# Attention with two feed-forward stages on one Trainium2 core: the second stage's w_in product by seven products instead of eight

## The chip, the cores and the metric

The kernel runs on one core of a Trainium2 chip. The time is the device time of one execution in microseconds (us); three executions were timed, and one more was profiled. TensorE (PE) multiplies, VectorE (DVE) and ScalarE (ACT) work elementwise, GpSimd (POOL) takes column maxima in the attention, and SyncE (SP) issues all DMAs, in program order.

## What is computed

A gated sum of causal attention and a memory read (4 batches, 8 heads, 576 tokens, head width 64) gives 2,304 tokens of width 512. Two feed-forward stages follow, all in float32:

```python
a = x @ w1
b = x @ w2
h = a * b @ w3
x = h @ w_out              # first stage: 512 -> 1024 -> 1024 -> 512

h = x @ w_in               # second stage: 512 -> 2048
sp = log1p(exp(h))
g = h * tanh(sp)           # Mish
return g @ w_out           # 2048 -> 512
```

## The kernel before

Everything is recorded first as a list of operations (`op`, line 104), each with an engine, a cost and the buffers that it reads and writes. `Recorder.schedule` (line 140) then sets the order: it plays the list through with the planner's costs, and on each engine takes the ready operation with the best key. On TensorE the key is the place in the record, plus `GB` = 300 for fill work; on the others it weighs the length of the chain that hangs on an operation against the place in the record. Buffers are given by name (tag) from rings of fixed length (`BUFS`, line 343); an operation that opens a buffer waits until the ring has one free. The order that comes out is fixed in the program: each engine, and the DMA queue of SP, goes through its list in order.

SBUF is divided in rooms. R1 and A1 serve the attention and the first feed-forward stage; R2 and A2 take their space when those are done (`rec.follow`, lines 1096 and 1105). A2 (tags f, s) opens when the attention ends, R2 when the first stage ends.

Every float32 operand is split in two float32r tiles, a rounded part H and the rest L, and one product is three matmuls (H·H, H·L, L·H in `HL`, line 768). The split is a cast on ScalarE and a subtraction on VectorE (`split`, line 875; `lo`, line 379). The weights of the second stage come as 64-bit numbers: a raw load of 512 KB into a buffer s, then one operation on ScalarE and two on VectorE turn 128 rows into float32 (`conv`, line 737; `conv2`, line 864). Two such row groups make one pair i of 8 (`NP2`).

The second stage works on chunks of 256 tokens (`CT`), 9 of them (`NC`). For each chunk and each pair i:

- an **h block** (`h_blk`, line 913) multiplies the activations of the chunk with pair i of w_in: 2 row groups x 4 parts of the depth x 3 matmuls of 256 columns = 24 matmuls into one PSUM bank;
- a **g block** (`g_blk`, line 929) takes Mish from PSUM (ScalarE), forms three sums and differences (VectorE), and splits the seven pieces that result (one cast, one subtraction of 896 columns);
- an **out block** (`fin`, line 946) multiplies them with w_out. It already uses seven products of half-size blocks in place of eight: 7 x 3 = 21 matmuls of 256 columns (`PRODUCTS`, line 944), summed over the pairs in four banks. `combine` (line 884) forms the combinations of w_out for it, four operations of 256 columns on VectorE and two splits (1,024 and 768 columns) per pair, in the first chunk.

h blocks and out blocks alternate on TensorE, the out block `LA` = 2 pairs behind. When a chunk is complete, `out_blk` (line 962) puts its four banks together and stores 2 x 256 KB. `load_x2` (line 899) loads and splits the next chunk's activations from DRAM (x2d).

The loads for this stage are recorded between the last units of the first stage (lines 1097 to 1104): 16 row groups of w_out and the first 10 of w_in, then 6 more beside the splits of w_in. All converted weights stay in SBUF in the ring f of 13.

Of the kernel before, what the change touches and what calls it, by code (L numbers as in the profile page):

```python
# [8 lines left out]
F32 = mybir.dt.float32  # L9
F32R = mybir.dt.float32r  # L10
# [276 lines left out]
def t_mm(n, m=128):  # L287
    return max(n * 0.4545 + 2, m * 0.834 + 2)
# [9 lines left out]
def kernel(  # L298
# [53 lines left out]
    ROOMS = {"x": R1, "u": R1, "t": R1, "f": A2, "s": A2, "G": R2, "H": R2, "ob": R2, "m": R2}  # L352
# [521 lines left out]

    def split(n, a, H, L):
        act(n, lambda: fl(H), lambda: fl(a), [a], [H])
        lo(n, lambda: fl(L), lambda: fl(a), lambda: fl(H), [a, H], [L])

    def split_in(i):
        for d in (WH, WL):  # L880
            d[i] = buf("wE" if i < 2 else "wB" if i < 6 else "wD", [P, 2, 512], F32R)
        split(1024, WC[i], WH[i], WL[i])

    def combine(i):

        c, m = LC[i], buf("ob", [P, 3, 256])
# [5 lines left out]
        HC[i] = buf("wA", [P, 2, 512], F32R)  # L892
        LL[i] = buf("f", [P, 2, 512], F32R)
        split(1024, c, HC[i], LL[i])
        for y, d in enumerate((HM, LM)):
            d[i] = buf("m" if 2 * i + y < BUFS["m"] else "f", [P, 3, 256], F32R)
        split(768, m, HM[i], LM[i])

    def load_x2(c):
        t0 = c * CT  # L900
        need = [x for x in range(2 * B) if x * HS < t0 + CT and (x + 1) * HS > t0]
        xc[c] = []
# [10 lines left out]
    def h_blk(c, i):  # L913
        ps = gbuf()
        w = (WH[i], WL[i])
        for y in range(2):
            for j in range(KD // 2):

                def f(y=y, j=j):
                    for k in range(2):  # L920
                        for z, (a, b) in enumerate(HL):
                            kk = 2 * j + k
                            mm(ps.tile[:, y * CT:(y + 1) * CT], w[a].tile[:, y, kk * P:(kk + 1) * P], xc[c][j].tile[:, b, k * CT:(k + 1) * CT],
                               kk == z == 0, kk == KD - 1 and z == 2)

                op("pe", 6 * t_mm(CT), f, r=[WH[i], WL[i], (xc[c][j], 0), (xc[c][j], 1)], w=[ps])
        return ps

    def g_blk(ps):
        G = buf("G", [P, 8, P])  # L930
        H = buf("H", [P, 2, 7 * P], F32R)
# [7 lines left out]
        act(7 * P, lambda: H.tile[:, 0], g7, [(G, 0), (G, 1)], [(H, 0)])  # L939
        lo(7 * P, lambda: H.tile[:, 1], g7, lambda: H.tile[:, 0], [(G, 0), (G, 1), (H, 0)], [(H, 1)])  # L940
        return H


# [168 lines left out]
    load_x2(0)
    NC = NT // CT
    for c in range(NC):
        acc = [gbuf() for _ in range(4)]
        gts = {}
        LA = CFG["LA"]
        for i in range(NP2 + LA):
            if i < NP2:
                if c == 0:  # L1120
                    combine(i)
                ps = h_blk(c, i)
            if i >= LA and (c < NC - 1 or i < NP2 + LA - 2):
                fin(i - LA, gts.pop(i - LA), acc)
            if i < NP2:
                gts[i] = g_blk(ps)
            if i == NP2 - 1 and c + 1 < NC:
                load_x2(c + 1)
        for part in (PRODUCTS[:6], PRODUCTS[6:]):
            for i in sorted(gts):  # L1130
                fin(i, gts[i], acc, part)
        out_blk(c, acc)
# [56 lines left out]
```

## Time and profile before

| | us |
|---|---|
| runs shown: 942.35, 942.94, 940.69; median | 942.35 |
| the profiled execution | 944.09 |
| its span, first to last instruction | 942.3 |
| TensorE busy in the span | 928.4 |
| VectorE busy | 675.6 |
| ScalarE busy | 536.4 |
| second stage, from TensorE's first h matmul to the end of the span | 551.5 to 942.3 |

The span is what the profile's rows count from; the execution's own time is 1.8 us longer. A matmul's recorded duration (281 ns for 256 columns) is longer than the distance to the next one, since they are pipelined: durations of TensorE are read from starts. The same holds, less so, on VectorE and ScalarE.

### The profile page before, as it was taken

How to read it: one execution, taken by the hardware profiler on the slowest of the kernel's cores; microseconds unless marked ns; L12 is line 12 of the kernel's file. 1: busy time of each engine (PE TensorE's matmuls, PEld its weight loads, DVE VectorE, ACT ScalarE, POOL GpSimd, SP SyncE). 2: the span in 40 equal slices, each digit the busy share in tenths (PEclk: the TensorE clock that was granted, in tenths of full speed). 3: DMA queues.
4: the chain of work that ended last, by engine and by line, in shares of the span. 5: the costliest groups of instructions: out<-in, count | busy, mean ns of one | idle time of the engine just before them, and what ended most of it. 6: DMA issues, size and time to landing. Idle time of an engine off the chain costs nothing.

```text
span 942.3 us, 17917 instructions
## 1 busy us (share of the span) xinstructions
PE 928.4 (99%) x6936; PEld 872.1 (93%) x6936; DVE 675.6 (72%) x1574; ACT 536.4 (57%) x1070; POOL 83.8 (9%) x70
## 2 busy tenths in 40 slices
PE   9999999999999999999999999999999999999998
PEld 7455888899899999999999999999999999999997
DVE  8989998999898988987367949844444454545453
ACT  6679967888787877866255745433233333333232
POOL 2111112322211112120000000000000000000000
PEclk9999999999999999999999999999999999999999
DMA  9788563543433522311299400000001010100000
GB/s 320 263 259 292 172 178 115 178 109 94 132 91 104 146 74 85 109 28 52 64 301 328 145 26 24 19 28 23 24 23 46 1 46 1 46 23 24 1 24 23
DMA packets 50341, 95.21 MB, mean 101 GB/s; under 512 B 10992, under 2 KB 27920, under 8 KB 50256
## 3 DMA queue, kind: packets, MB, share of 16 engines
q1 hardware_dynamic: 50256, 94.07, 31.3%
q8 instruction: 54, 0.88, 0.4%
q14 instruction: 31, 0.25, 0.1%
HBM read 84.28 MB, written 9.77 MB: 100 GB/s over the span
## 4 chain that ended last, share of the span: by engine, by line
PE 76%; DVE 10%; DMA 6%; ACT 5%; issue 2%; SPq 0%; POOL 0%; DVEq 0%; ACTq 0%
PE g L367 76%; DMA Rr<-d 3%; DVE t L385 2%; DVE QK L370 2%; DMA d<-cp 1%; DVE mnl L385 1%; DVE e L385 1%; ACT t L377 1%; DVE e L370 1%; DVE g L624 1%; ACT u L750 1%; DVE x L370 1%; ACT e L377 1%; DMA cp<-d 1%; DMA ld<-in_qk_dram 1%
## 5 line engine op out<-in xcount | busy, mean ns | idle before, releaser
L370 DVE TENSOR_TENSOR H<-G,H 128x896 fp32r<-128x896 f32 x72 | 78.7, 1092 | 97.3 <-ACT H L375 97.3
L385 DVE TENSOR_TENSOR t<-g,t 128x288 f32<-128x288 f32 (+6 forms) x344 | 121.2, 380 | 21.1 <-PE g L367 17.2
L375 ACT CAST H<-G 128x896 fp32r<-128x896 f32 x72 | 67.9, 943 | 119.1 <-PE g L367 99.4
L367 PE MATMUL g<-wA,H 128*128 128x256 f32 x576 | 135.6, 281 | 0.0
L385 DVE TENSOR_TENSOR G<-G 128x128 f32<-128x128 f32 (+1 forms) x216 | 72.4, 335 | 60.3 <-ACT G L934 55.8
L644 POOL PARTITION_ALL_REDUCE t<-t x64 | 83.1, 1307 | 351.4 <-DVE t L385 293.5
L367 PE MATMUL g<-f,H 128*128 128x256 f32 x477 | 111.7, 280 | 0.0
L367 PE MATMUL g<-x,wB 128*128 128x288 f32 x768 | 109.8, 296 | 0.5 <-DVE e L385 0.5
L367 PE MATMUL g<-u,wA 128*128 128x288 f32 x768 | 110.2, 298 | 0.0
L367 PE MATMUL g<-s,wB 128*128 128x256 f32 x864 | 109.5, 282 | 0.0
L367 PEld LDWEIGHTS g<-s,wB 128*128 128x128 f32 x864 | 106.1, 188 | 0.0
L367 PEld LDWEIGHTS g<-x,wB 128*128 128x128 f32 x768 | 104.4, 188 | 1.2 <-DVE e L385 0.7
L367 PEld LDWEIGHTS g<-u,wA 128*128 128x128 f32 x768 | 104.2, 188 | 1.3 <-ACT R L375 0.2
L367 PEld LDWEIGHTS g<-wA,H 128*128 128x128 f32 x576 | 103.0, 189 | 0.0
L934 ACT ACTIVATE G<-g 128x512 f32<-128x512 f32 x72 | 43.0, 597 | 95.0 <-PE g L367 87.7
L367 PE MATMUL g<-e,V 128*65 128x320 f32 (+12 forms) x576 | 89.3, 302 | 2.5 <-DVE t L385 1.3
L367 PEld LDWEIGHTS g<-e,V 128*65 128x65 f32 (+1 forms) x576 | 66.3, 136 | 19.8 <-issue 2.2
L367 PE MATMUL g<-m,H 128*128 128x256 f32 x459 | 83.1, 281 | 0.0
L367 PEld LDWEIGHTS g<-f,H 128*128 128x128 f32 x477 | 82.1, 188 | 0.0
L367 PEld LDWEIGHTS g<-m,H 128*128 128x128 f32 x459 | 66.9, 188 | 0.0
L367 PE MATMUL g<-wB,wD 128*128 128x512 f32 x128 | 59.5, 603 | 2.8 <-DVE wB L754 1.4
L367 PE MATMUL g<-x,wE 128*128 128x288 f32 x384 | 55.8, 300 | 1.1 <-DVE t L385 0.9
(121 smaller groups left out, 1553.4 us busy)
## 6 DMA issues: line engine op xcount, KB each, us to landing
ld<-in_qk_dram SPq DMA_DIRECT2D x24, 608.0 KB
u<-in_moe_w_dram SPq DMA_DIRECT2D x26, 512.0 KB
s<-in_moe_w_out_dram SPq DMA_DIRECT2D x16, 512.0 KB
s<-in_moe_w_in_dram SPq DMA_DIRECT2D x16, 512.0 KB
Rr<-d SPq DMA_DIRECT2D x24, 288.0 KB
x2d<-t SPq DMA_DIRECT2D x16, 288.0 KB
s<-x2d SPq DMA_DIRECT2D x18, 256.0 KB
out_dram<-ob SPq DMA_DIRECT2D x18, 256.0 KB
```

What stands on the lines that cost most here:

```text
L367: nc.tensor.matmul(out=o, lhsT=lhsT, rhs=rhs, start=start, stop=stop)
L370: eng.tensor_tensor(out=o, in0=a, in1=b, op=ALU.subtract)
L375: op("act", t_act(n, psum), lambda: nc.scalar.copy(out=o(), in_=i()), r, w)
L377: op("act", t_act(n, psum) + more, lambda: nc.scalar.activation(out=o(), in_=i(), func=func, **kw), r, w)
L385: op(eng, t_dve(n) if eng == "dve" else t_pool(n), lambda: e.tensor_tensor(out=o(), in0=a(), in1=b(), op=alu), r, w)
L624: nc.vector.tensor_tensor(out=o, in0=o, in1=mv, op=ALU.add)
L644: op("pool", 430 + 2.6 * (b - a), lambda mv=mv: nc.gpsimd.partition_all_reduce(mv(), mv(), P, bass_isa.ReduceOp.max), r=[(m, x)], w=[(m, x)])
L750: op("act", t_act(512) + 100, lambda: nc.scalar.activation(out=lw(), in_=top(), func=AF.Identity, scale=2.0 ** -5, bias=frac), r=[(raw, 0) ...
L934: op("act", t_act(512, True), lambda: nc.scalar.activation(out=G.tile[:, 0:4].rearrange("p a b -> p (a b)"), in_=ps.tile, func=AF.Mish, sc ...
```

## The change

w_in too is now multiplied by seven products of half-size blocks, two chunks of 256 tokens at a time. Nine chunks are odd, so the first 256 tokens go through the old h block, and the other 2,048 in four chunks of 512 (`NS` = 4).

- `split_sums` forms four sums and differences of a pair of w_in and splits them (tiles SH, SL), beside the pair's own split.
- `load_x2s` loads 512 tokens of activations, forms four differences of 512 columns and splits seven factors (tags r and b).
- `h_seven` is a **step**: for one chunk of 512 and one pair, seven products of 2 x 3 = 6 matmuls of 256 columns into four banks; then one copy on ScalarE and four additions on VectorE (three of 512 columns, one of 256) give h in a buffer G, one Mish of 1,024 columns follows, and `store_g` writes G to DRAM.
- Both products are no longer interleaved: all steps run first, then all 72 out blocks. `g_blk` loads its 256 KB of g from DRAM, and does the rest as before.
- SBUF no longer holds all weights: `keep` writes a converted pair to DRAM, `fetch` loads it again. Kept are all 8 pairs of w_out and pairs 5 to 7 of w_in. `combine` writes the splits of w_out over the buffers that the same pair of w_in had.

The core of the diff:

```diff
-        "f": 13, "s": 4, "G": 2, "H": 2, "ob": 1, "m": 11, **CFG.get("BUFS", {}),
+        "f": 5, "s": 4, "q": 8, "b": 8, "r": 4, "G": 2, **CFG.get("BUFS", {}),
...
+    def split_sums(i, o):
+        c = WC[i]
+        for x, y, z, alu in ((3, (c, 2), (c, 3), ALU.add), (2, (c, 0), (c, 2), ALU.subtract), (0, (o, 3), (c, 0), ALU.subtract), (1, (c, 1), (o, 0), ALU.subtract)):
+            tt(256, lambda x=x: quarter(o, x), lambda y=y: quarter(*y), lambda z=z: quarter(*z), alu, [c, o], [o])
+        for d in (SH, SL):
+            d[i] = buf(side(i), [P, 2, 512], F32R)
+        split(1024, o, SH[i], SL[i])
+
+    def keep(to, src, i, swap):
+        for y in range(2):
+            conv2(to, src, i, y, 1 - y if swap else y)
+        d = ld[swap, i] = Buf(dram, [P, 1024], F32, f"kept{swap}_{i}", 1)
+        c = to[i]
+        dma(lambda: d.tile, lambda: fl(c), 524288, r=[c], w=[d])
...
+    FACTORS = [(0, 0, 0, 0), (0, 1, 1, 0), (1, 0, 1, 1), (1, 2, 2, 0), (1, 3, 2, 1), (0, 3, 3, 0), (1, 1, 3, 1)]
+
+    def h_seven(c, i, then=()):
+        G = buf("G", [P, 4, CT])
+        bank = [gbuf() for _ in range(4)]
+        for x, (d, qd, k, half) in enumerate(FACTORS):
...
+                for kk in range(2):
+                    for z, (a, b) in enumerate(HL):
+                        mm(bank[k].tile[:, CT * half:CT * half + CT], quarter(w[a], qd)[:, kk * P:kk * P + P], xc[c][x].tile[:, b, kk * CT:kk * CT + CT],
+                           kk == z == 0, kk == 1 and z == 2)
+            op("pe", 6 * t_mm(CT), f, r=[w[0], w[1], (xc[c][x], 0), (xc[c][x], 1)], w=[bank[k]])
+            if x < len(then):
+                then[x]()
...
+        act(CT, lambda: o(0), lambda: bank[0].tile[:, 0:CT], [bank[0]], [G], True)
+        tt(512, lambda: o(1, 3), lambda: pair(1), lambda: wide(0), ALU.add, [bank[1], G], [G])
+        tt(512, lambda: o(0, 4, 3), lambda: pair(2), lambda: wide(2), ALU.add, [bank[2], G], [G])
+        tt(CT, lambda: o(2), lambda: bank[2].tile[:, CT:512], lambda: o(0), ALU.add, [bank[2], G], [G])
+        tt(512, lambda: o(0, 4, 3), lambda: pair(3), lambda: o(0, 4, 3), ALU.add, [bank[3], G], [G])
+        op("act", t_act(1024), lambda: nc.scalar.activation(out=fl(G), in_=fl(G), func=AF.Mish, scale=2.0 ** -8), [G, table], [G])
+        store_g(c, i, G, 1024)
+
+    def g_blk(c, i):
+        G = buf("r", [P, 8, P])
+        H = [buf("b", [P, 7 * P], F32R) for _ in range(2)]
...
+        dma(lambda: G.tile[:, 0:4].rearrange("p a b -> p (a b)"), lambda: d.tile[:, 512 * y:512 * y + 512], 262144, r=[d], w=[(G, 0)])
...
+    loads = [lambda i=i: keep(LC, moe2_w_out, i, 1) for i in range(NP2)]
+    loads += [lambda i=i: keep(WC, moe2_w_in, i, 0) for i in range(BUFS["f"], NP2)]
+    loads += [lambda i=i, y=y: conv2(WC, moe2_w_in, i, y) for i in range(BUFS["f"]) for y in range(2)]
+    loads += [load_x2]
+    loads += [lambda i=i: split_sums(i, buf("s", [P, 2, 512])) for i in range(4)]
...
+    for i in range(NP2):
+        h_blk(i)
+        if i == 2:
+            for f in load_x2s(1):
+                f()
+        if i >= 4:
+            split_sums(i, WC[i])
+    for c in range(1, NS + 1):
+        for i in range(NP2):
+            h_seven(c, i, more[pre:] if c < NS and i == NP2 - 1 else ())
...
+            if c == NS:
+                combine(i)
...
+    work = [(c, i) for c in range(NC) for i in range(NP2)]
+    for n in range(len(work) + LA):
+        if n < len(work):
+            gts[n] = g_blk(*work[n])
...
+        if c < NC - 1 or i < NP2 - 2:
+            fin(i, gts.pop(n - LA), accs[c])
+            if i == NP2 - 1:
+                out_blk(c, accs[c])
```

What the planner makes of it at three places. First TensorE, from the first stage's last 96 products on (u and wA; s: activations, wE, wB, wD: w_in; H, f, m: the out product's operands). Before:

```order
L367 MATMUL g<-u,wA 128x288 x96
L367 MATMUL g<-s,wE 128x256 x48
L367 MATMUL g<-s,wB 128x256 x36
L367 MATMUL g<-wA,H 128x256
L367 MATMUL g<-f,H 128x256
L367 MATMUL g<-wA,H 128x256 x2
```

Now, with b for the factors of the activations and q for the split sums of w_in:

```order
L367 MATMUL g<-u,wA 128x288 x96
L367 MATMUL g<-s,wE 128x256 x48
L367 MATMUL g<-s,wB 128x256 x96
L367 MATMUL g<-s,wD 128x256 x48
L367 MATMUL g<-b,wE 128x256 x12
L367 MATMUL g<-b,q 128x256 x18
L367 MATMUL g<-b,wE 128x256 x6
L367 MATMUL g<-b,q 128x256 x6
```

The out products have left this place; the eight h blocks of the first chunk stand together, and steps of 42 products follow.

Second, SP's queue in the stage where the weights are loaded (kept: the copies in DRAM; x2d: the activations' array in DRAM):

```order
+L364 DMA s<-in_moe_w_in_dram 128x1024
+L364 DMA kept_6_6982<-f 128x1024
+L364 DMA s<-in_moe_w_in_dram 128x1024 x3
+L364 DMA kept_7_7053<-f 128x1024
+L364 DMA s<-in_moe_w_in_dram 128x1024 x2
 L364 DMA s<-x2d 128x2x256 x2
```

Stores now stand between the raw loads, and the first chunk's activations (the last row) behind all of them; before, the raw loads stood here without stores.

Third, VectorE around the change from steps to out blocks (G_9488: additions of the last chunk's seventh step; 128x896: the split of a g block; f_9218, wD and s_9452: pair 6 of w_out; r: a g block's sums):

```order
L370 TENSOR_TENSOR b_9533<-r_8602,b_9054 128x896
L385 TENSOR_TENSOR G_9488<-g_9499,G_9488 128x2x256
L385 TENSOR_TENSOR s_9452<-f_9218,s_9452 128x256
L370 TENSOR_TENSOR b_9561<-r_9052,b_9541 128x896
L385 TENSOR_TENSOR s_9574<-f_9297 128x256
L385 TENSOR_TENSOR f_9297<-f_9297 128x256
L370 TENSOR_TENSOR b_9585<-r_9064,b_9570 128x896
L370 TENSOR_TENSOR wD_9602<-f_9218,wD_9583 128x1024
L370 TENSOR_TENSOR b_9619<-r_9075,b_9595 128x896
```

The combinations and splits of w_out, which stood beside the first chunk's h and out blocks, now stand between the last additions and the first g blocks' splits.

## Rows read from the trace of the kernel before

**Rows 1.** The page: its first line, and busy time by engine.
```profile
span 942.3 us, 17917 instructions
...
PE 928.4 (99%) x6936; PEld 872.1 (93%) x6936; DVE 675.6 (72%) x1574; ACT 536.4 (57%) x1070; POOL 83.8 (9%) x70
```
**Rows 2.** Chain of waits from 440 us on: start, duration in us, what.
```profile
439.93 496.26 PE g L367 x4074
```
**Rows 3.** Timeline of PE around the start of the second stage: start, duration.
```profile
551.52 5.92 PE L367 MATMUL g<-s,wE 128*128 128x256 f32 x48
```
**Rows 4.** Timeline of TensorE's weight loads (PEld), 701 to 708 us.
```profile
701.91 2.95 PEld L367 LDWEIGHTS g<-s,wB 128*128 128x128 f32 x24
704.79 0.19 PEld L367 LDWEIGHTS g<-wA,H 128*128 128x128 f32 x1
...
707.26 2.95 PEld L367 LDWEIGHTS g<-s,wD 128*128 128x128 f32 x24
```
**Rows 5.** Timeline of SP's queue, 440 to 610 us: DMAs issued.
```profile
476.19 18.47 SPq L364 DMA_DIRECT2D s<-in_moe_w_out_dram  x12
...
516.64 7.15 SPq L364 DMA_DIRECT2D s<-in_moe_w_in_dram  x4
527.40 5.71 SPq L364 DMA_DIRECT2D s<-x2d  x4
```
**Rows 6.** Windows: stretch, length, busy us by engine, clock, DMA share, GB/s.
```profile
476.00:484.00 8.00, 8.00 (x63) 8.00 (x62) 6.01 (x13) 4.87 (x11) 0.00 (x0) 1.00 0.88 303
...
524.00:532.00 8.00, 8.00 (x63) 8.00 (x62) 7.97 (x15) 6.50 (x13) 0.00 (x0) 1.00 0.43 137
```
**Rows 7.** Timeline of DVE, 568 to 573 us, operations without idle time between.
```profile
568.25 0.42 DVE L385 TENSOR_TENSOR ob<-f 128x256 f32<-128x256 f32 x1
568.59 0.28 DVE L385 TENSOR_TENSOR G<-G 128x128 f32<-128x128 f32 x1
568.79 0.41 DVE L385 TENSOR_TENSOR ob<-f,ob 128x256 f32<-128x256 f32 x1
569.12 1.22 DVE L370 TENSOR_TENSOR f<-f,wA 128x1024 fp32r<-128x1024 f32 x1
570.26 0.95 DVE L370 TENSOR_TENSOR m<-ob,m 128x768 fp32r<-128x768 f32 x1
571.13 1.08 DVE L370 TENSOR_TENSOR H<-G,H 128x896 fp32r<-128x896 f32 x1
572.13 0.41 DVE L385 TENSOR_TENSOR ob<-f 128x256 f32<-128x256 f32 x1
```
**Rows 8.** Timeline of DVE, 533 to 536 us.
```profile
533.59 0.68 DVE L370 TENSOR_TENSOR s<-s 128x512 fp32r<-128x512 f32 x1
534.20 0.45 DVE L385 TENSOR_TENSOR t<-g,t 128x288 f32<-128x288 f32 x1
534.56 0.68 DVE L370 TENSOR_TENSOR s<-s 128x512 fp32r<-128x512 f32 x1
```
**Rows 9.** Windows in the second stage: the first chunks, and a later one.
```profile
560.00:580.00 20.00, 20.00 (x170) 20.00 (x169) 18.04 (x35) 11.73 (x16) 0.00 (x0) 1.00 0.00 1
...
800.00:840.00 40.00, 40.00 (x338) 40.00 (x337) 19.41 (x36) 12.81 (x18) 0.00 (x0) 1.00 0.08 28
```
**Rows 10.** Groups by line and shape, 600 to 900 us: busy us, mean ns.
```profile
L969 DVE SCALAR_TENSOR_TENSOR ob<-g,ob 128x512 f32<-128x512 f32 x24 | 16.6, 692 | 14.8 <-ACT ob L377 9.4 <-PE g L367 3.7
...
L377 ACT ACTIVATE ob<-g 128x256 f32<-128x256 f32 x8 | 3.1, 384 | 15.9 <-PE g L367 15.9
...
L375 ACT CAST wA<-f 128x1024 fp32r<-128x1024 f32 x1 | 1.1, 1050 | 2.2 <-DVE f L385 2.2
```
**Rows 11.** Timeline of SP's queue at the end: the last two stores of 256 KB.
```profile
938.57 0.82 SPq L364 DMA_DIRECT2D out_dram<-ob  x2
```
**Rows 12.** Windows at the end, columns as in rows 6.
```profile
939.20:939.60 0.40, 0.00 (x0) 0.00 (x0) 0.00 (x0) 0.00 (x0) 0.00 (x0) 1.00 0.48 179
...
940.40:940.80 0.40, 0.00 (x0) 0.00 (x0) 0.00 (x0) 0.00 (x0) 0.00 (x0) 0.74 0.96 364
```

More of the change, by code (lines that the diff above doesn't have):

```diff
@@ L862, with conv2 @@
     WC, WH, WL, LC, HC, LL, HM, LM, xc = {}, {}, {}, {}, {}, {}, {}, {}, {}
-    def conv2(d, src, i, y):
+    SH, SL, ld, gd = {}, {}, {}, {}
+    NC = NT // CT
+    NS = NC // 2
+    def conv2(d, src, i, y, rows=None):
         if y == 0:
             d[i] = buf("f", [P, 2, 512])
-        conv(src[(2 * i + y) * P:(2 * i + y + 1) * P, :], lambda: buf("s", [P, 512, 2], I32), d[i], y, table, kind="f2")
+        r0 = (2 * i + (y if rows is None else rows)) * P
+        conv(src[r0:r0 + P, :], lambda: buf("s", [P, 512, 2], I32), d[i], y, table, kind="f2")
     def fl(b):
@@ L891, in combine, with from_x2, load_x2 @@
             tt(256, o, a, b, ALU.subtract, [c, m], [c, m])
-        HC[i] = buf("wA", [P, 2, 512], F32R)
-        LL[i] = buf("f", [P, 2, 512], F32R)
+        for d in (HC, LL):
+            d[i] = buf(main(i), [P, 2, 512], F32R)
         split(1024, c, HC[i], LL[i])
-        for y, d in enumerate((HM, LM)):
-            d[i] = buf("m" if 2 * i + y < BUFS["m"] else "f", [P, 3, 256], F32R)
+        for d in (HM, LM):
+            d[i] = buf(side(i), [P, 3, 256], F32R)
         split(768, m, HM[i], LM[i])
[L899 to L902, printed above, removed]
+    def from_x2(t0, n):
+        return [x for x in range(2 * B) if x * HS < t0 + n and (x + 1) * HS > t0]
+    def load_x2():
         raw = buf("s", [P, 2, 2 * CT])
         for j in range(KD // 2):
-            dma(lambda j=j: raw.tile[:, j].rearrange("p (i t) -> p i t", i=2), lambda j=j: x2d[2 * j * P:(2 * j + 2) * P, t0:t0 + CT].rearrange("(i p) t -> p i t", p=P),
-                1024 * CT, r=[(fx2[x], 2 * j + 1) for x in need], w=[(raw, j)])
+            dma(lambda j=j: raw.tile[:, j].rearrange("p (i t) -> p i t", i=2), lambda j=j: x2d[2 * j * P:(2 * j + 2) * P, 0:CT].rearrange("(i p) t -> p i t", p=P),
+                1024 * CT, r=[(fx2[x], 2 * j + 1) for x in from_x2(0, CT)], w=[(raw, j)])
+        xc[0] = []
         for j in range(KD // 2):
@@ L910, in load_x2, with load_x2s, diff, factor @@
             lo(512, lambda xx=xx: xx.tile[:, 1], lambda j=j: raw.tile[:, j], lambda xx=xx: xx.tile[:, 0], [(raw, j), (xx, 0)], [(xx, 1)])
-            xc[c].append(xx)
-    def h_blk(c, i):
+            xc[0].append(xx)
+    def load_x2s(c):
+        t0 = (2 * c - 1) * CT
+        raw = [buf("r", [P, 2, 2 * CT]) for _ in range(2)]
+        T = buf("r", [P, 2, 2 * CT])
+        for j in range(2):
+            dma(lambda j=j: raw[j].tile, lambda j=j: x2d[2 * j * P:(2 * j + 2) * P, t0:t0 + 2 * CT].rearrange("(i p) t -> p i t", p=P),
+                2048 * CT, r=[(fx2[x], 2 * j + 1) for x in from_x2(t0, 2 * CT)], w=[raw[j]])
+        B11, B12, B21, B22 = [((raw[j], t), lambda j=j, t=t: raw[j].tile[:, :, t * CT:t * CT + CT]) for j in range(2) for t in range(2)]
+        T1, T2 = [((T, y), lambda y=y: T.tile[:, y].rearrange("p (i t) -> p i t", i=2)) for y in range(2)]
+        xc[c] = []
+        def diff(o, a, b):
+            tt(2 * CT, o[1], a[1], b[1], ALU.subtract, [a[0], b[0], o[0]], [o[0]])
+        def factor(a):
+            xx = buf("b", [P, 2, 2 * CT], F32R)
+            v = lambda y: xx.tile[:, y].rearrange("p (i t) -> p i t", i=2)
+            act(2 * CT, lambda: v(0), a[1], [a[0]], [(xx, 0)])
+            lo(2 * CT, lambda: v(1), a[1], lambda: v(0), [a[0], (xx, 0)], [(xx, 1)])
+            xc[c].append(xx)
+        diff(T1, B12, B11)
+        diff(T2, B22, T1)
+        diff(B12, B22, B12)
+        def second_t4():
+            diff(B11, B21, T2)
+            factor(B11)
+        return [lambda a=a: factor(a) for a in (B11, B21, T2, B12, T1)] + [second_t4, lambda: factor(B22)]
+    def store_g(c, i, G, n):
+        d = gd[c, i] = Buf(dram, [P, n], F32, f"gd{c}_{i}", 1)
+        dma(lambda: d.tile, lambda: fl(G)[:, 0:n], 512 * n, r=[G], w=[d])
+    def h_blk(i):
         ps = gbuf()
@@ L927, in h_blk @@
[L927 to L931, printed above, removed]
+                op("pe", 6 * t_mm(CT), f, r=[WH[i], WL[i], (xc[0][j], 0), (xc[0][j], 1)], w=[ps])
+        G = buf("G", [P, 4, CT])
+        op("act", t_act(512, True), lambda: nc.scalar.activation(out=fl(G)[:, 0:512], in_=ps.tile, func=AF.Mish, scale=2.0 ** -8), [ps, table], [G])
+        store_g(0, i, G, 512)
+    FACTORS = [(0, 0, 0, 0), (0, 1, 1, 0), (1, 0, 1, 1), (1, 2, 2, 0), (1, 3, 2, 1), (0, 3, 3, 0), (1, 1, 3, 1)]
@@ new lines, in h_seven, with f @@
+    def h_seven(c, i, then=()):
+        G = buf("G", [P, 4, CT])
+        bank = [gbuf() for _ in range(4)]
+        for x, (d, qd, k, half) in enumerate(FACTORS):
+            w = ((WH, WL), (SH, SL))[d]
+            w = (w[0][i], w[1][i])
+            def f(x=x, w=w, qd=qd, k=k, half=half):
+                for kk in range(2):
[5 more added lines that the diff above has]
+                then[x]()
+        o = lambda a, b=None, s=1: G.tile[:, a:b:s] if b else G.tile[:, a]
+        pair = lambda k: bank[k].tile.rearrange("p (a b) -> p a b", b=CT)
+        wide = lambda k: o(k).unsqueeze(1).to_broadcast([P, 2, CT])
+        act(CT, lambda: o(0), lambda: bank[0].tile[:, 0:CT], [bank[0]], [G], True)
[5 more added lines that the diff above has]
+        store_g(c, i, G, 1024)
@@ L938, in g_blk @@
         tt(P, lambda: g(7), lambda: g(3), lambda: g(6), ALU.subtract, [(G, 0), (G, 1)], [(G, 1)])
[L939 to L940 removed]
+        act(7 * P, lambda: H[0].tile, g7, [(G, 0), (G, 1)], [H[0]])
+        lo(7 * P, lambda: H[1].tile, g7, lambda: H[0].tile, [(G, 0), (G, 1), H[0]], [H[1]])
         return H
@@ L954, in f @@
                 o = acc[bank].tile[:, DH * half:DH * half + DH]
-                gh, gl = (H.tile[:, y, k * P:(k + 1) * P] for y in range(2))
+                gh, gl = (x.tile[:, k * P:(k + 1) * P] for x in H)
                 mm(o, gh, quarter(U, qd), i == 0 and first, False)
@@ L958, in f @@
                 mm(o, gl, quarter(U, qd), False, i == NP2 - 1 and last)
-            op("pe", 3 * t_mm(DH), f, r=[(H, 0), (H, 1), L, U], w=[(acc[bank], half)])
+            op("pe", 3 * t_mm(DH), f, r=[H[0], H[1], L, U], w=[(acc[bank], half)])
     def out_blk(c, acc):
-        ob = buf("ob", [P, 4, DH])
+        ob = buf("G", [P, 4, DH])
         o = lambda a, b=None, s=1: ob.tile[:, a:b:s] if b else ob.tile[:, a]
@@ L1101 @@
         if n >= CFG["F2N"] and loads:
-            conv2(*loads.pop(0))
+            loads.pop(0)()
     for x in loads:
-        conv2(*x)
+        x()
     rec.follow(R2)
@@ L1107 @@
         split_in(i)
-        if i < 3:
-            for y in range(2):
-                conv2(WC, moe2_w_in, i + 5, y)
+        if i + BUFS["f"] < NP2:
+            fetch(WC, i + BUFS["f"], 0)
     op("act", 1400, lambda: None, w=[table])
[L1112 to L1132, printed above, removed]
+    for i in range(NP2):
[8 more added lines that the diff above has]
+            h_seven(c, i, more[pre:] if c < NS and i == NP2 - 1 else ())
+            if c < NS and i == NP2 - 2:
+                more = load_x2s(c + 1)
+                pre = BUFS["b"] - 7
+                for f in more[:pre]:
+                    f()
+            if c == NS - 1 and i >= NP2 - BUFS["f"]:
+                fetch(LC, i - NP2 + BUFS["f"], 1)
+            if c == NS:
+                combine(i)
+                if i + BUFS["f"] < NP2:
+                    fetch(LC, i + BUFS["f"], 1)
+    LA = CFG["LA"]
+    work = [(c, i) for c in range(NC) for i in range(NP2)]
+    gts, accs = {}, {}
+    for n in range(len(work) + LA):
+        if n < len(work):
+            gts[n] = g_blk(*work[n])
+        if n < LA:
+            continue
+        c, i = work[n - LA]
+        if i == 0:
+            accs[c] = [gbuf() for _ in range(4)]
+        if c < NC - 1 or i < NP2 - 2:
+            fin(i, gts.pop(n - LA), accs[c])
+            if i == NP2 - 1:
+                out_blk(c, accs[c])
+    for part in (PRODUCTS[:6], PRODUCTS[6:]):
+        for n in sorted(gts):
+            fin(work[n][1], gts[n], accs[NC - 1], part)
+    out_blk(NC - 1, accs[NC - 1])
     rec.flush()
```

23 lines of the change are left out of this document (14 added, 9 removed).

## The prediction

> **What bounds the kernel now.** I read the page first, then the chain of waits, then the stage that the change touches, engine by engine. The page gives TensorE (PE) 928.4 us of a span of 942.3 [rows 1]. The chain of waits says the same more sharply: from 439.93 to 936.19 it is one single piece, 4,074 TensorE products in a row, and only the last 6 us belong to VectorE (DVE) and the final store [rows 2]. The second feed-forward stage begins at 551.52, right behind the first one's last product [rows 3]. So whatever shortens TensorE's list there shortens the kernel, as long as nothing else becomes later than TensorE.
>
> Two prices for TensorE come from the weight loads, whose starts are sharp: an h block of 24 products runs from 701.91 to 704.79, 2.88 us or 0.120 each; the out block of 21 that follows runs to 707.26, 2.47 us or 0.1176 each [rows 4].
>
> **The change, term by term.**
>
> *TensorE.* Before: 9 chunks x 8 weight pairs x 24 = 1,728 products for h. After: one chunk of 256 tokens as before (8 x 24 = 192), and 4 chunks of 512 tokens x 8 x 7 x 6 = 1,344; together 1,536. The out products stay at 72 x 21. Removed are 192 products of 256 columns: 192 x 0.120 = **23.0 us less**. The new products are sums of six with a new half bank after each, where the old ones were sums of twelve. If they run at the out block's pace, another 1,344 x 0.0024 = 3.2 us go. I take 0.120, the row that has the same operands in the same roles, and keep 26.2 for the lower end.
>
> *Loads ahead of the stage.* The weights of the second stage no longer all stay in SBUF: 11 converted pairs of 512 KB (eight of w_out, three of w_in) are written to DRAM between the loads and fetched later. Before, 28 raw loads are issued from 476.19 to the end of the last group at 523.79: 47.6 us, 1.70 each [rows 5], with the DMA engines busy 0.88 where that stretch begins and 0.43 right behind it [rows 6]. The stretch is bound by transfers, so the stores lengthen it. Two stores of 256 KB alone on the queue keep the engines busy from 939.4 to 940.8, 1.4 us for 512 KB [rows 12]; at a load's price it is 1.70. The raw loads then end at 523.8 + 15.4 to 18.7 = 539.2 to 542.5. The first activations go out behind them; before, their load and split took from the issue at 527.40 to 535.24, 7.8 us [rows 5, 8], which gives 547.0 to 550.3. TensorE wants them at 551.52. I charge **nothing**, covered by the first stage's last products; the margin is only 1.2 to 4.5 us. The other end: a store holds one of five buffers until it has landed, and the next pair is converted into that buffer. Were each store to stand in the path for its whole 3.73 us (issue at 938.57, end of the span at 942.3 [rows 1, 11]), the stretch would grow by 41.0 us instead of 18.7, and TensorE would wait 550.3 + 22.3 - 551.5 = 21.1 us.
>
> *VectorE while h is made.* A step of a 512-token chunk lasts 42 x 0.120 = 5.04 us on TensorE. VectorE puts the seven products together in three additions of 512 and one of 256. Back to back, VectorE starts an operation 0.34 us after one of 256 elements, 0.20 after 128, 1.14 after 1,024, 0.87 after 768, 1.00 after 896 [rows 7], 0.61 after 512 [rows 8]. So a step costs it 3 x 0.61 + 0.34 = 2.17 us of 5.04, and seven splits and four differences of the next activations (11 x 0.61 = 6.7 us per eight steps) fit beside it. Nothing on the path. The splits of the weight sums of pairs 0 to 3 come before TensorE's first new step, those of 4 to 7 (4 x (4 x 0.34 + 1.14) = 10.0 us) beside the 23.0 us of the first chunk, on a VectorE that was already busy 18.04 of 20 us here without stopping TensorE [rows 9].
>
> *ScalarE (ACT) and the store of g.* Each step ends with one Mish of 1,024 and a 512 KB store; two buffers take turns. From a landed store the next use of the buffer needs a copy (0.38), the additions (2.17), Mish (taken as 1.05, the cast of the same size [rows 10]), about 0.4 for hand-overs, and the store's landing (3.73 at the end of the kernel [rows 1, 11]): 7.7 us, against two steps, 10.1. Covered by 2.4 us.
>
> *The change of stage.* The split of a w_out pair writes into buffers that the same pair of w_in leaves, so it can't start before that pair's last product. From the first product of the last chunk to the end of eight out blocks TensorE has 8 x 5.04 + 8 x 2.47 = 60.1 us. In it VectorE has 8 x 2.17 = 17.4 for the additions, 8 x (1.14 + 0.87) = 16.1 for splits, 16 x 0.34 = 5.4 for the combinations of four pairs (the order puts those of the other four in an earlier chunk), and ten g blocks, each 2 x 0.20 + 0.34 + 1.00 = 1.74, 17.4: in all 56.3. Its first step has little to do, so 55.1 are to be had. I charge **1.0 us**.
>
> *The out stage.* An out block takes 2.47 on TensorE; VectorE needs 1.74 and an eighth of a chunk's recombination, (3 x 0.61 + 0.34) / 8 = 0.27: 2.01. Before, blocks came every 5.35 us and VectorE was half idle, 19.41 of 40 us [rows 9]. It now carries 81%. A g load has four buffers of 2.47 us each, 9.9; its turn is at most 3.73 for landing, 0.74 for the sums, 1.05 for a cast, 1.00 for the split and about 0.6 of hand-overs, 7.1. Covered. The end is as before: the last blocks' order is kept.
>
> **Sum.** The profiled execution took 944.09: 944.09 - 23.0 + 1.0 = 922.1. It lies 1.74 above the median of the three runs, so against that I predict **920.3 us**.
>
> **A rule weighed.** In the rows VectorE starts the next operation 0.07 to 0.09 us before the recorded duration of the last one is over (0.42 long, 0.34 to the next start [rows 7]); I used the starts. The Trainium skill (VectorE: DVE Perf Modes, Terms) says that a flush follows every VectorE operation and that the next can't issue until the pipe is empty. By that rule the whole durations would count, as in the first rival; the starts in this trace speak against it.
>
> **Rivals.**
> 1. *VectorE decides the change of stage.* With whole durations (0.69 or 0.68 for 512, 0.42, 0.28, 1.22, 0.95, 1.08 [rows 7, 8, 10]): 8 x 2.49 + 8 x 2.17 + 16 x 0.42 + 10 x 2.06 = 64.6, which is 9.5 over 55.1. Later blocks, at 2.37 of 2.47, still hide. Time: 942.35 - 23.0 + 9.5 = 928.9. For it: hand-overs between ScalarE and VectorE in fixed order, which I priced at nothing there. Against: the starts in rows 7, and TensorE kept full in rows 9.
> 2. *The first h block waits for its activations.* Up to the 21.1 us above: 920.3 + 21.1 = 941.4, no change. For it: the thin margin, and SP, which issues in order and so queues loads behind stores. Against: the engines are idle a tenth of that stretch, which stores can use [rows 6].
> 3. *Slower: the store of g sets the step.* With two buffers a step can't be shorter than half of (4.0 + landing time). It decides from a landing time of 6.1 us on; each us more costs 0.5 x 32 = 16 us, and from 7.5 us the gain is gone. At 8.5 the kernel takes 920.3 + 38.7 = 959.0. For it: in the crowded stretch twelve loads take 18.47 us through four buffers [rows 5], 6.2 us a turn, just at that point. Against: in the h stage one store in 5.04 us asks the engines for 1.4, and the uncrowded landing is 3.73. The Trainium skill (DMA: Bandwidth & Descriptors, Anatomy of one DMA) warns that completion can take surprisingly long where the target is HBM; it gives no length for it.
>
> That the change does something else can be left out: the order shows 192 old and 1,344 new products.
>
> **Chances.** Forecast 0.74, rival 1 0.12, rival 2 0.08 (half of it reaching past the 0.3% that a measurement of this kernel can tell from no change, that is 2.8 us, short of a gain), rival 3 0.06. So faster 0.90, same 0.04, slower 0.06. The range runs from 942.35 - 26.2 = 916.1, the faster pace without any wait, up to rival 1's end: 916 to 929; rival 3 and the longer part of rival 2 are left out.
>
> **What would show it.** Right: TensorE without a gap from the first stage into the second, the first new step some 23 us later, steps of 5.04 us, out blocks of 2.47 from about 736 on, VectorE at eight tenths to the end. Wrong: a gap on TensorE at 551 whose releaser is the split of the activations (rival 2); gaps at the first out blocks released by VectorE's splits (rival 1); steps longer than 5.04 us with ScalarE's copy waiting for a store of g (rival 3). A gap in the out stage with VectorE waiting for g loads would break a step I priced at nothing.

## The result, and the profile after

The changed kernel takes **919.76 us** (median of 4 runs), the kernel before in the same comparison 942.64: ratio 0.9759, 95% interval 0.9742 to 0.9776, 22.9 us less. The forecast was 920.3 (916 to 929). In a second set, beside 941.72 of the kernel before, it took 917.68, ratio 0.9746 (0.973 to 0.9762). The profiled execution took 918.72 with a span of 916.9.

The page, as rows 1:
```profile
span 916.9 us, 18264 instructions
...
PE 904.6 (99%) x6744; PEld 848.7 (93%) x6744; DVE 773.5 (84%) x1770; ACT 554.7 (60%) x1090; POOL 84.4 (9%) x70
```
TensorE has 192 instructions fewer and 23.8 us less work, VectorE 97.9 us more; the span, 25.4 us shorter, goes with TensorE. The chain of waits from 430 us on, as rows 2:
```profile
429.90 481.06 PE g L367 x3941
```
It is still one piece of products, now ending at 910.96. Nowhere behind 440 us does TensorE wait. Its timeline around the start of the stage, as rows 3:
```profile
536.65 12.95 PE L367 MATMUL g<-u,wA 128*128 128x288 f32 x96
549.44 5.92 PE L367 MATMUL g<-s,wE 128*128 128x256 f32 x48
```
From the start of the stage to the end of the chain it is 936.19 - 551.52 = 384.67 us before and 910.96 - 549.44 = 361.52 after: **23.15 less**. That the stage begins 2.1 us earlier is kept apart: in eight profiles of the changed kernel and its variants (all but the last one below) it begins anywhere between 548.25 and 550.68. Of the kernel before there is one profile, so whether a part of the 2.1 belongs to the change is open; the medians, 22.9 us apart here and 24.0 in the second set, leave about 1 us for it at most. The variants are compared by the stage's length too.

The pace, from the weight loads. First the kernel before, from the first product of one chunk's h blocks to the next one's (the second border is the last row of rows 4, 707.26):
```profile
664.39 0.79 PEld L367 LDWEIGHTS g<-s,wD 128*128 128x128 f32 x6
```
The same in the changed kernel: three borders of 512-token chunks with the middle of the first one, and two out blocks that are eight apart with the one in the middle:
```profile
612.38 0.79 PEld L367 LDWEIGHTS g<-b,wE 128*128 128x128 f32 x6
...
632.26 1.50 PEld L367 LDWEIGHTS g<-b,wB 128*128 128x128 f32 x12
...
652.41 0.67 PEld L367 LDWEIGHTS g<-b,wE 128*128 128x128 f32 x5
...
692.44 0.67 PEld L367 LDWEIGHTS g<-b,wE 128*128 128x128 f32 x5
...
752.47 0.67 PEld L367 LDWEIGHTS g<-wE,b 128*128 128x128 f32 x5
...
762.40 0.78 PEld L367 LDWEIGHTS g<-wB,b 128*128 128x128 f32 x6
...
772.47 0.67 PEld L367 LDWEIGHTS g<-wE,b 128*128 128x128 f32 x5
```
Before: 42.87 us for 8 x (24 + 21) = 360 products, 0.1191 each. After: 40.03 us for 8 x 42 = 336, 0.1191 each, and 20.00 for 8 x 21 = 168, 0.1190 each. At this mean, 192 products are 22.9 us.

It is a mean of two paces, though, before and after. Before, the h blocks take 0.1200 a product (207.4 us for the stage's 1,728, added up from start to start) and the out blocks 0.1181, close to what rows 4 show of one pair. After, the four steps of pairs 0 to 3, whose split sums lie in q, take 19.88 us (612.38 to 632.26, 0.1183 a product), those of pairs 4 to 7 20.15 (0.1199); four out blocks 9.93 and 10.07 (752.47, 762.40, 772.47). What makes the one pace or the other, no run here shows. Over the stage the h products cost 207.4 before and 192 x 0.1200 + 1,344 x 0.1191 = 183.1 after, 24.2 less; the 1,512 out products went from 0.1181 to 0.1190 each, 1.4 more. That makes 22.8, as from the first product to the start of the last (385.80 and 363.02 us); the rest of the 23.15, 0.4, is the place at the end where the chain leaves TensorE.

The load stretch. SP's queue at its end, and windows as in rows 6:
```profile
530.71 3.33 SPq L364 DMA_DIRECT2D s<-in_moe_w_in_dram  x2
535.01 0.89 SPq L364 DMA_DIRECT2D s<-x2d  x2
```
```profile
476.00:484.00 8.00, 8.00 (x62) 8.00 (x62) 6.67 (x15) 4.76 (x10) 0.00 (x0) 1.00 0.98 335
484.00:492.00 8.00, 8.00 (x63) 8.00 (x62) 6.03 (x13) 4.23 (x9) 0.00 (x0) 1.00 0.99 360
...
500.00:508.00 8.00, 8.00 (x62) 8.00 (x61) 4.37 (x9) 2.83 (x6) 0.00 (x0) 1.00 1.02 391
...
524.00:532.00 8.00, 8.00 (x62) 8.00 (x62) 7.33 (x14) 6.10 (x11) 0.00 (x0) 1.00 0.72 223
```
The raw loads that began at 476.19 before (rows 5) begin at 474.11 and end at 534.04: 59.9 us where it was 47.6, 12.3 more for 11 stores, 1.12 each. The share of the DMA engines is 0.98 to 1.03 from 476 to 524 where it was 0.88 to 0.92. From 524 to 532 it is 0.72: just ahead, from 520.4 to 524.35, SP's queue stands still until VectorE has converted a load and its buffer is free. So the 1.12 is a mean over a stretch that transfers bind for the most part, not throughout. The split of the activations, on VectorE:
```profile
542.43 1.29 DVE L370 TENSOR_TENSOR s<-s 128x512 fp32r<-128x512 f32 x2
```
It ends at 543.7, 5.7 us before TensorE wants it.

The change of stage and the out stage, windows as in rows 9 (behind the length stand the busy us of TensorE, its weight loads, VectorE, ScalarE and POOL, then granted clock, DMA share, GB/s):
```profile
696.00:736.00 40.00, 40.00 (x338) 40.00 (x337) 39.76 (x71) 25.26 (x32) 0.00 (x0) 1.00 0.49 169
736.00:756.00 20.00, 20.00 (x170) 20.00 (x169) 19.96 (x42) 10.26 (x12) 0.00 (x0) 1.00 0.41 128
756.00:776.00 20.00, 20.00 (x170) 20.00 (x169) 18.91 (x41) 7.90 (x10) 0.00 (x0) 1.00 0.41 136
776.00:816.00 40.00, 40.00 (x338) 40.00 (x337) 35.49 (x75) 16.21 (x19) 0.00 (x0) 1.00 0.41 133
```
VectorE is busy 59.7 of the first 60 us, TensorE loses nothing. VectorE's timeline there:
```profile
732.24 1.08 DVE L370 TENSOR_TENSOR b<-r,b 128x896 fp32r<-128x896 f32 x1
733.24 1.22 DVE L370 TENSOR_TENSOR wD<-f,wD 128x1024 fp32r<-128x1024 f32 x1
734.37 1.09 DVE L370 TENSOR_TENSOR b<-r,b 128x896 fp32r<-128x896 f32 x1
735.38 0.29 DVE L385 TENSOR_TENSOR r<-r 128x128 f32<-128x128 f32 x1
...
749.30 1.08 DVE L370 TENSOR_TENSOR b<-r,b 128x896 fp32r<-128x896 f32 x1
```
Starts are 1.00 to 1.01 apart after 896 elements and 1.13 after 1,024, each less than the duration recorded. The last row, ending at 750.4, is the g block for the out block that starts at 752.47: about 2 us in hand, the tightest place of the stage.

ScalarE's timeline and its waits from 545 us on (what waited for what; total, times, longest):
```profile
657.66 1.06 ACT L1027 ACTIVATE G<-G 128x1024 f32<-128x1024 f32 x1 [3.80 <-DVE G L385]
659.19 1.06 ACT L1027 ACTIVATE G<-G 128x1024 f32<-128x1024 f32 x1 [0.47 <-DVE G L385]
662.08 0.37 ACT L375 COPY G<-g 128x256 f32<-128x256 f32 x1 [1.83 <-DMA gd<-G]
```
```profile
ACT G L375 <- DMA gd<-G: 16.0, 10, 3.4
```
The copy waits for the store that followed the first Mish (ended 658.72): it took 3.4 us to land. Such waits occur ten times, with 2.7 to 5.4 us from the Mish to the copy, and none of them reaches TensorE.

### The profile page after: what moved, and what is told of

Same layout as the page of the kernel before. It is cut to its first block, busy times and chain, and to the rows that moved or that the text cites. A ratio compares the mean times of both kernels' runs of the same rounds, so it can differ in the third digit from the quotient of the medians.

```text
span 916.9 us, 18264 instructions
## 1 busy us (share of the span) xinstructions
PE 904.6 (99%) x6744; PEld 848.7 (93%) x6744; DVE 773.5 (84%) x1770; ACT 554.7 (60%) x1090; POOL 84.4 (9%) x70
## 4 chain that ended last, share of the span: by engine, by line
PE 78%; DVE 10%; ACT 5%; DMA 4%; issue 2%; SPq 0%; POOL 0%; DVEq 0%; ACTq 0%
PE g L367 78%; DMA Rr<-d 2%; DVE t L385 2%; DVE QK L370 2%; DMA d<-cp 1%; ACT t L377 1%; DVE mnl L385 1%; DVE e L385 1%; DVE e L370 1%; ACT u L750 1%; ACT e L377 1%; DVE g L624 1%; DVE x L370 1%; DMA d<-R 1%; ACT mnl L375 0%
## 5 line engine op out<-in xcount | busy, mean ns | idle before, releaser
L375 ACT CAST b<-r 128x896 fp32r<-128x896 f32 (+1 forms) x100 | 83.6, 851 | 115.0 <-PE g L367 68.8
L370 DVE TENSOR_TENSOR b<-r,b 128x896 fp32r<-128x896 f32 (+1 forms) x100 | 96.3, 975 | 18.8 <-ACT b L375 18.2
L385 DVE TENSOR_TENSOR G<-g,G 128x512 f32<-128x512 f32 (+1 forms) x128 | 77.8, 619 | 31.8 <-PE g L367 24.2
L385 DVE TENSOR_TENSOR r<-r 128x128 f32<-128x128 f32 (+2 forms) x232 | 79.1, 355 | 3.0
L367 PE MATMUL g<-wB,b 128*128 128x256 f32 x432 | 68.7, 281 | 0.0
L367 PEld LDWEIGHTS g<-wB,b 128*128 128x128 f32 x432 | 58.8, 190 | 0.0
L367 PE MATMUL g<-x,wD 128*128 128x288 f32 x384 | 56.8, 297 | 0.0
L367 PE MATMUL g<-QK 128*128 128x320 f32 (+4 forms) x368 | 55.7, 289 | 1.1 <-DVE t L385 1.1
L367 PE MATMUL g<-wA,b 128*128 128x256 f32 x324 | 56.3, 283 | 0.0
L367 PE MATMUL g<-q,b 128*128 128x256 f32 x324 | 56.1, 281 | 0.0
```

The costliest lines, as they stand in the source:

```text
L370: eng.tensor_tensor(out=o, in0=a, in1=b, op=ALU.subtract)
L375: op("act", t_act(n, psum), lambda: nc.scalar.copy(out=o(), in_=i()), r, w)
L385: op(eng, t_dve(n) if eng == "dve" else t_pool(n), lambda: e.tensor_tensor(out=o(), in0=a(), in1=b(), op=alu), r, w)
```

## The experiments

The prediction's theory: TensorE's 192 products are the whole gain, everything else is covered. Its rivals, turned into edits: VectorE decides, the loads decide, the store of g decides. Lengths of the second stage, read from the chains as above:

| kernel | median us | ratio to before (95%) | stage, us | against the changed |
|---|---|---|---|---|
| before | 942.23 / 941.72 | | 384.67 | +23.15 |
| changed, first profile | 919.76 | 0.9759 (0.9742 to 0.9776) | 361.52 | 0 |
| changed, second set | 917.68 | 0.9746 (0.973 to 0.9762) | 361.51 | 0 |
| an eighth product | 941.75 | 0.9999 (0.9988 to 1.001) | 384.56 | +23.0 |
| g block, +0.34 on VectorE | 920.93 | 0.9778 (0.9762 to 0.9794) | 363.44 | +1.9 |
| g block, +0.68 | 940.68 | 0.9982 (0.9973 to 0.9991) | 382.30 | +20.8 |
| w_out split twice | 927.27 | 0.9845 (0.9829 to 0.9862) | 368.58 | +7.1 |
| G stored twice | 919.5 | 0.9759 (0.9742 to 0.9775) | 362.17 | +0.7 |
| G stored three times | 937.33 | 0.9947 (0.9927 to 0.9966) | 380.70 | +19.2 |
| kept pairs stored twice | 929.49 | 0.987 (0.9846 to 0.9894) | 372.66 | +11.1 |

The first four variants stand against the first before, the others and the second set's run of the change against the second; the first profile's before is 942.64. The last one's stage is counted from 549.56, 0.13 us behind the start of the first stage's last product, as it begins in the others. In the one with +0.68 the chain leaves TensorE through ScalarE, 0.7 us earlier than elsewhere: from the first to the last product its stage is 21.5 longer, where the other lengths agree with the table.

**1. The eighth product given back.** Each step of the 512-token chunks multiplies once more, into the half of bank 0 that nobody reads.
```diff
+            if x == 0:
+                op("pe", 6 * t_mm(CT), lambda w=w: f(0, w, qd=0, k=0, half=1), ...)
```


> The changed kernel with an eighth product in each of the 32 steps: six more matmuls of 256 columns into the unused half of the step's first bank, read by nobody. All else, the way through DRAM included, stays. My theory (the gain is the 192 removed matmuls at 0.119 us, everything else is hidden): 22.9 us more than the changed kernel's 919.8, about 942.7, level with the kernel before. Rival (taking the two products apart and sending g through DRAM brings or costs something of its own): a time off 942.7 by that amount, 3 us or more. Steps should take 48 x 0.119 = 5.72 us.

Measured: 941.75, no difference from before, and the stage's length comes back to 0.1 us. All that the change adds (stores, fetches, 200 VectorE operations) is still there, and TensorE waits for none of it. The two changes of pace are in it too, and offset each other (h 1.2 us less, out 1.4 more). To within some 0.3 us the gain is the 192 products.

**2 and 3. VectorE in the out stage.** The g block's subtraction of 256 elements is repeated, once and twice.
```diff
+        tt(2 * P, lambda: G.tile[:, 5:7], lambda: G.tile[:, 0:5:4], ..., ALU.subtract, ...)
```


> Each g block's subtraction of 256 columns on VectorE is done twice (the second writes the same values). By starts VectorE needs 2.01 + 0.34 = 2.35 us a block in the out stage, under TensorE's 2.50: no change there, and at most 10 x 0.34 less some 2 us of margin = 1.4 us at the change of stage: 919.8 to 921.2. By whole durations (a flush between operations) it needs 2.37 + 0.42 = 2.79: 0.29 x 72 = 21 us more, 941.

> The same subtraction three times, 0.68 us more per block. By starts 2.01 + 0.68 = 2.69 against 2.50: 0.19 x 62 = 11.8 us in the out stage and 10 x 0.68 - 2 = 4.8 at the change of stage, 16.6 in all: about 936, with gaps on TensorE that VectorE ends. By whole durations 3.21 a block: 0.71 x 72 = 51, about 971. If VectorE had much more room than I priced: 920.

Measured: 920.93 and 940.68. Windows from 800 to 840 us, of the one and of the other:
```profile
800.00:840.00 40.00, 40.00 (x337) 39.95 (x336) 37.93 (x89) 15.11 (x18) 0.00 (x0) 1.00 0.41 132
```
```profile
800.00:840.00 40.00, 38.05 (x307) 36.63 (x307) 38.95 (x95) 14.38 (x18) 0.00 (x0) 1.00 0.35 111
```
With one more operation VectorE is busy 95% of the time and TensorE all but full: of the stage's 1.9 us 1.3 are lost at the change of stage (755 to 759), the rest in delays of some 0.1 us later. By whole durations (2.37 + 0.42 = 2.79 us for a block of 2.50) TensorE would have lost 0.29 x 72 = 21 us. With two more it is VectorE that sets the pace: the chain alternates between its lines, with a block every 2.78 us (eight from 796.95 to 819.20 on TensorE). The starts add up to 2.01 + 0.68 = 2.69. Of the other 0.09, 0.07 is the idle 2.6% of the window: two pauses of 0.48 us, each ended by TensorE, one in eight blocks. That is the term by which the expectation of the third kernel, about 936, came out too low: with 0.28 a block in place of 0.19 its sum is 62 x 0.28 + 4.8 = 22.2, where 20.8 to 21.5 were lost. Added up from start to start, VectorE's load comes out right to 3% even where VectorE sets the pace.

**4. VectorE at the change of stage.** VectorE's half of the 1,024-element split of each w_out pair (in `combine`) is done twice there, eight times 1.14 us, 9.1 in all.
```diff
         split(1024, c, HC[i], LL[i])
+        lo(1024, lambda: fl(LL[i]), lambda: fl(c), lambda: fl(HC[i]), [c, HC[i]], [LL[i]])
```


> At the change of stage the split of 1,024 columns of each w_out pair is done twice on VectorE: 8 x 1.14 = 9.1 us more, all between the first product of the last chunk and the eighth out block. Theory (VectorE is full there and has about 2 us of margin, read from the splits of the g blocks that end 2.0 us before TensorE wants them): about 7 us more, 927, with a gap on TensorE at the first out blocks. Rival (VectorE has room there, the change of stage is nowhere near its limit): 920, no gap.

Measured: 927.27, the stage 7.1 us longer. Windows, as above:
```profile
740.00:760.00 20.00, 15.71 (x114) 14.72 (x113) 20.00 (x37) 7.99 (x10) 0.00 (x0) 0.94 0.16 54
760.00:780.00 20.00, 20.00 (x167) 20.00 (x167) 18.91 (x42) 9.49 (x12) 0.00 (x0) 0.98 0.51 169
```
```profile
758.00:760.00 2.00, 2.00 (x12) 2.00 (x11) 2.00 (x5) 1.81 (x3) 0.00 (x0) 0.50 0.36 126
```
Of 9.1 us, 2.0 were hidden: that is the reserve which the trace showed at 750. TensorE loses the rest between 748 and 761, with VectorE busy all the time. Of it 4.3 us are recorded idle time. Some 1.5 are half a clock: after its two longest waits TensorE runs from about 757.4 to 760.9 at a granted 0.50 (1.2 GHz), 15 products 0.213 us apart. The last 1.3 lie at the waits themselves, where a product's recorded duration covers part of the pause. That clock hides behind VectorE, though. The split that stood 2 us ahead of its out block ends at 760.37 here (stage beginning 1.06 later), and the block starts at 760.57; at full clock TensorE would have waited for it. Experiment 2 agrees: ten to twelve g blocks x 0.34 = 3.4 to 4.1, less 2.0, is 1.4 to 2.1, and 1.3 of its 1.9 us are lost here.

**5 and 6. The store of g.** Every step's G goes to DRAM a second, and a third time, where nobody reads it (shown is the third; the other variant has no loop).
```diff
         store_g(c, i, G, 1024)
+        for y in range(2):
+            d = Buf(dram, [P, 1024], F32, f"more{y}_{c}_{i}", 1)
+            dma(lambda d=d: d.tile, lambda: fl(G), 524288, r=[G], w=[d])
```


> Every step of the 512-token chunks stores its G twice, the second time into DRAM that nobody reads: 32 more stores of 512 KB. The prediction's ring (two rooms, 4.0 us of work between a landed store and the next one's issue, then the landing) gives half of 4.0 + landing. In the trace of the changed kernel ScalarE's copy that waits for a store goes on 3.4 us after the Mish before that store; one more transfer of 1.4 makes 4.8, with the 3.73 of the prediction 5.1, so 4.4 to 4.6 us a step, under TensorE's 5.00: no change, 919.8. If a store's landing is already at its limit, each us more costs 0.5 x 32 = 16 us: 936 or more.

> The same with two more stores a step, three in all. By the ring: landing 3.4 + 2.8 = 6.2 to 3.73 + 2.8 = 6.5, half of 4.0 + that is 5.1 to 5.27 us a step where TensorE needs 5.00, so 0.1 to 0.27 x 32 = 3 to 9 us more, 923 to 929, with ScalarE's copy waiting for a store of G ahead of TensorE's waits. By transfers alone (3 x 1.4 = 4.2 of 5.0 us a step) nothing changes: 919.8. Were the point at which rival 3 decides lower than the 6.1 us of the prediction, more than 930.

Twice: 919.5, and the stage is 0.7 us longer; the rest of the 1.8 between the medians lies outside it (the profiled executions are 3.3 apart, 2.3 of it ahead of the stage). ScalarE waits for stores oftener, TensorE hardly (waits of ScalarE from 560 to 745, of TensorE from 420 us):
```profile
ACT G L375 <- DMA more<-G: 32.4, 17, 3.7
```
```profile
PE g L367 <- DVE G L385: 0.2, 1, 0.2
```
Three times: 937.33, past the forecast of 923 to 929. The chunks start at 572.59, 612.61, 656.99 and 700.97, the out blocks at 750.83: 40.0, 44.4, 44.0 and 49.9 us. ScalarE's timeline in the third chunk:
```profile
676.37 1.06 ACT L1027 ACTIVATE G<-G 128x1024 f32<-128x1024 f32 x1 [2.87 <-DVE G L385]
...
683.15 0.37 ACT L375 COPY G<-g 128x256 f32<-128x256 f32 x1 [1.54 <-DMA more<-G]
686.38 1.06 ACT L1027 ACTIVATE G<-G 128x1024 f32<-128x1024 f32 x1 [2.86 <-DVE G L385]
```
The store of the first row's G is issued at 677.46 and its last copy has landed at 683.15: 5.7 us; the next one takes from 681.64 to 688.39, 6.75. From a copy to the issue of its store it is 4.3. Half of 4.3 + 5.7 to 6.75 is 5.0 to 5.5 us a step, and the two middle chunks took 5.5 (in the latter of them some 1.4 us are half a clock: after a wait the granted clock is 0.50 from 658.8 to 662.2). So the ring of the prediction is real, and its point of decision (6.1 us of landing) was about right. The landings that ScalarE waited for, 5.3 to 7.3 us over these two chunks, lie around the 6.2 to 6.5 of the expectation; the 4.0 before them is 4.3, and the half clock was not in it. About half of the 19.2 us is of another kind: in the last chunk 9.8 us are lost rather than 4.2, and there steps that come late meet a VectorE without slack. That link wasn't tried apart.

**7. The load stretch.** Each of the 11 kept pairs is written twice.
```diff
         dma(lambda: d.tile, lambda: fl(c), 524288, r=[c], w=[d])
+        d2 = Buf(dram, [P, 1024], F32, f"again{swap}_{i}", 1)
+        dma(lambda: d2.tile, lambda: fl(c), 524288, r=[c], w=[d2])
```


> Each of the 11 converted weight pairs that are written to DRAM ahead of the stage is written twice (the second copy is read by nobody): 11 x 1.4 to 1.54 = 15.4 to 16.9 us more of transfers in a stretch whose DMA engines are already fully busy. In the changed kernel the activations' last split ends 5.7 us before TensorE wants it, so by the prediction's account (loads covered by a margin, rival 2 beyond it) the first h block now comes 9.7 to 11.2 us late: 929.5 to 931. If the stores lie beside the loads for nothing, or the margin is larger than it looks, 919.8; if each store stands in the path for its whole landing of 3.7 us, 11 x 3.7 - 5.7 = 35 us, 955.

Measured: 929.49. The first products of the stage on TensorE, and windows of 2 us there (the two numbers behind POOL's column are the granted clock and the DMA share):
```profile
555.16 0.58 PE L367 MATMUL g<-s,wE 128*128 128x256 f32 x1 [5.43 <-ACT s L375]
558.09 8.53 PE L367 MATMUL g<-s,wE 128*128 128x256 f32 x47 [2.36 <-DVE s L370]
566.46 11.68 PE L367 MATMUL g<-s,wB 128*128 128x256 f32 x96
```
```profile
551.00:553.00 2.00, 0.00 (x0) 0.00 (x0) 1.28 (x3) 0.58 (x1) 0.00 (x0) 1.00 0.20 45
553.00:555.00 2.00, 0.00 (x0) 0.00 (x0) 1.51 (x2) 2.00 (x4) 0.00 (x0) 0.72 1.05 361
555.00:557.00 2.00, 0.58 (x1) 0.28 (x1) 1.78 (x4) 0.72 (x2) 0.00 (x0) 0.50 0.96 289
...
563.00:565.00 2.00, 2.00 (x14) 2.00 (x14) 2.00 (x4) 1.75 (x3) 0.00 (x0) 0.72 0.97 355
565.00:567.00 2.00, 2.00 (x19) 2.00 (x18) 1.94 (x5) 0.34 (x1) 0.00 (x0) 1.00 0.76 295
```
The activations' split ends at 558.6 instead of 543.7, so a further store costs the stretch 14.9 / 11 = 1.36 us (1.33 by the end of the raw loads). The margin is used up and TensorE waits 5.4 + 2.4 us: rival 2, made to happen. The time came out at the lower end of the forecast, and by luck: all but the first product of the first h block came 8.4 us late, where 9.7 to 11.2 were expected, and a part that was not in my account made up for it, the clock. TensorE stood idle, its granted clock fell from 1.00 to 0.50 (2.4 to 1.2 GHz) and came back at about 564, some 6 us after the engine was at work again. The 47 products take 8.37 us (558.09 to 566.46) instead of 5.6: 2.8 us, a third again on top of the wait.

## Why the prediction was right

The mechanism held: TensorE works from 440 us to the end of the chain without a wait, and three limits that were said to be covered were covered. The number is helped by parts that offset each other.

**TensorE's term** was 23.0; the stage is 23.15 shorter, and the eighth product put 23.0 back. The count decided. That the price fits so well is in part luck. Both prices read in rows 4 hold for the whole stage before (0.1200 and 0.1181), but the new products came at 0.1191: the h products alone saved 24.2, between the 23.0 and the 26.2 of the prediction. The out products, which the prediction left unchanged, slowed from 0.1181 to 0.1190 and gave 1.4 of it back.

**Loads**, priced at nothing with 1.2 to 4.5 us in hand: right, with 5.7 in hand. The price of a store, 1.40 to 1.70, was too high; it measured 1.12. That the stores partly filled the tenth of the engines' time that rows 6 show idle fits the shares, 0.88 to 0.92 before and 0.98 to 1.03 after up to 524 us, but wasn't tried apart. With the share near 1, a further store cost 1.36. The other end, 3.73 for each store, is far off.

**The change of stage** was charged 1.0 and cost 0, with 2.0 to spare, so VectorE's 56.3 against 55.1 were about 3 us too pessimistic. Which part of the 56.3 is too high, the runs don't tell. This 1.0 and the stage's early beginning, 2.1, are most of what lies between the 918.72 of the profiled execution and the 922.1 of the sum; the median, 919.76, is 0.5 below the forecast.

**VectorE by starts** (rival 1 refuted): experiment 2, with VectorE at 95%, lost 1.9 us where whole durations ask 21. The rule of the Trainium skill (VectorE: DVE Perf Modes, Terms), that the next operation can't issue until the pipe is empty, would have given that if an operation's recorded duration lasts until the pipe is empty. Read so, it is contradicted here as in rows 7: starts come 1.00 us apart behind durations of 1.08.

**The store of g** (rival 3): over the ten stores that ScalarE waited for, landing took 2.7 to 5.4 us, so with the 4.3 of experiment 6 the turn takes 7.0 to 9.7 of two steps, 10.0. The predicted 7.7 lies in that, from 4.0 and a single landing of 3.73; the 2.4 in hand were 0.3 in the slowest turn. Twice as many stores were free, three times were not. The Trainium skill (DMA: Bandwidth & Descriptors, Anatomy of one DMA) warns that completion can be slow where the target is HBM; a length it does give, a fixed 2.0 us or so, for DMAs issued from GpSimd. No run here separates completion from transfer: of the 5.7 to 6.75 us of three stores in a row an estimated 4.2 are transfers, at the 1.4 each of rows 12.

**The out stage** ran as costed: 2.50 us a block, VectorE busy 35.49 of 40 us, 89%. Predicted were 2.01 of 2.47, 81%, by starts; by whole durations a block has 2.37, 95%. The recorded share lies between the two: some operations follow each other at once, others have a pause behind them. That no g load delayed the stage shows in TensorE's waits: there are none.

## What to carry to other kernels

Where one engine is 99% busy and the chain is one piece of its work, count the instructions that go and price each kind by its own blocks, those that stay too: a whole period that mixes kinds gives only their mean (0.119 here, for 0.120 and 0.118). Then spend the effort on the reserves of whatever must stay hidden (here 2.0 us on VectorE at the change of stage, 5.7 on the loads, one more store per step). Sum an engine's load from start to start; here that held up to 95% of VectorE's time, and to 3% where VectorE set the pace. A covered wait that comes into the open on TensorE can cost more than its length: with the clock at 0.50 behind it, 7.8 us of waits cost 11.1 in experiment 7.

## What was not expected of the hardware

Stores between loads raised the DMA engines' share from 0.88 to 0.92 up to 0.98 to 1.03 for most of the stretch, and a store of 512 KB cost 1.12 us of it, less than the 1.36 of the next one. After 5.4 us of idle time the granted clock was 0.50 (1.2 GHz), and it was 0.50 through some 6 us of renewed work: 2.8 us. And products of the same shape, each with a weight load of its own, come 0.118 or 0.120 us apart over whole blocks and stages, and which of the two goes with the tiles that they read; what makes the difference is open.
